# A decode step with grouped-query attention: the queries made the stationary operand of the scores, and 46 units of on-chip store in place of 48

## The chip, the cores and the metric

One core of one Trainium2 chip. The metric is the device time of one execution in microseconds (us), median of several executions. Most executions of one kernel here lie within 0.3 us of their median, so a difference of 1 us is well seen. All runs compared below are of the fast state, but for one single run that is named.

## The reference

One token goes through a block: a conditioned layer norm, attention over a cache of 65,536 positions, a second norm and a small gated feed-forward. The attention is all of the traffic: K and V have 8 heads x 65,536 x 128 in bf16, 134 MB each.

```
Hq, Hkv, Sk, Dh, D = 32, 8, 65536, 128, 512
q = x @ wq                              # 32 heads, 4 of them to one K/V head
scores = einsum('bhqd,bhkd->bhqk', q, k) * Dh ** -0.5
p = softmax(scores)
o = einsum('bhqk,bhkd->bhqd', p, v)
out = o.reshape(...) @ wo
# around it: h = layernorm(x)*(1+c)+s, x += g * attention(h); then x += g2 * swiglu(h2), F = 1792
```

## The kernel before

K and V come in chunks of 16,384 positions: 32 of K and 32 of V, 4 MB each, 128 partitions of 32 KB. They land in `store`, a hand-managed area of 4 KB units a partition; a chunk takes eight units, so 48 units are six slots. A load is issued, in a fixed order, when its slot comes free.

```
UNITS = 48
S_LAG = 2
...
const = ctx.enter_context(tc.tile_pool(name="const", bufs=1))
small = ctx.enter_context(tc.tile_pool(name="small", bufs=2))
once = ctx.enter_context(tc.tile_pool(name="once", bufs=1))
spool = ctx.enter_context(tc.tile_pool(name="store", bufs=1))
...
store = spool.tile([P, UNITS * UNIT], BF16, name="store", tag="store")
...
def room(n):          # n units that start at a multiple of n
    fits = [u for u in range(0, UNITS - n + 1, n) if all(free[u:u + n])]
    ...
```

A bank is 1,024 positions of K. TensorE turns it (four transposes of 128x128 words of 32 bits, each a pair of bf16), ACT and DVE in turn copy it out of PSUM, and eight small matmuls make the scores: a block of K is the stationary operand, 8 columns of q move.

```
def emit_T(n):
    ...
    for e4 in range(4):
        nc.tensor.transpose(out=ktp[:, e4, :], in_=kt32[:, j0:j0 + 2, :]..., identity=ident_f[:])
    ...                                      # copy to kts on ACT or DVE
    if jb == BPC - 1:
        done(("k", n // BPC))                # the slot is free, next load

def emit_S(n):
    ...
    for e4 in range(4):
        for e in range(2):
            nc.tensor.matmul(out=st[:, b0:b0 + 2, :]..., lhsT=ktsv[:, e4, :, e], rhs=qpair[:, g, e, :, :]...,
                             start=(e == 0), stop=(e == 1))

def sm_exp(cc, negb, h):                     # four times a chunk, once for each head
    nc.scalar.activation(out=pt_of[cc][:, :, h], in_=st_of[cc][:, :, h], func=ACT.Exp, ...)
```

PV is 32 matmuls a chunk with 512 columns of V moving, in four column tiles of TensorE at a time. At the end of the stream come w_gate, w_up and w_down, and after w_down has landed only 56 matmuls (`f_ps`), a few small instructions and the store of the result are left.

## Time and profile before

| | before |
|---|---|
| time, median of 13 runs (range) | 683.99 us (683.84 to 684.35) |
| DMA queue q1, share of 16 engines' span | 97.9% |
| instruction fetches (q8) | 64 |
| TensorE waiting for K | 60.3 us |
| chunk of K, issue to landing | 43.7 us |

From the page of before: span and instructions, the busy time of the engines, and two lines of the part on DMA queues (packets, MB, and the time that their packets took as a share of 16 engines' span).

```profile
span 682.3 us, 18421 instructions
...
PE 569.4 (83%) x8259; PEld 500.6 (73%) x8259; DVE 262.8 (39%) x612; ACT 201.3 (30%) x527; POOL 3.6 (1%) x17
...
q1 hardware_dynamic: 12160, 285.48, 97.9%
q8 instruction: 64, 1.05, 0.6%
```

The data queue q1 is at work for 97.9% of the span, on average over the 16 engines: 0.979 x 682.3 = 668.0 us. This product is how long an average engine was at the data itself. 285.48 MB in 668.0 us is 427 GB/s. What the stream could reach at most was not shown; but the packets of 32 KB, which carry 268 of the 285 MB, took 1221.0 ns on average and 1213 ns at the least, so by that measure only 0.7% is left in them (an estimate).

The table of stretches for before: start and end in us, their length, then busy us (and instructions) of each engine, the granted clock of TensorE, the mean busy share of the 16 DMA engines, GB/s.

```profile
core 0: us, PE busy (x) PEld busy (x) DVE busy (x) ACT busy (x) POOL busy (x), PEclk, DMA share, GB/s
20.00:660.00 640.00, 553.90 (x7877) 486.29 (x7878) 255.15 (x566) 197.74 (x520) 0.00 (x0) 0.85 1.00 428
...
665.00:677.00 12.00, 6.27 (x163) 5.80 (x159) 2.39 (x14) 0.42 (x2) 0.55 (x1) 0.50 0.55 224
```

From 20 to 660 us the mean share is 1.00: the DMA engines do not run dry. In the last 12 us it is 0.55: about half of the engines have finished, and the kernel waits for the others. That is the tail.

The waits of TensorE in before (engine, line, what it waited for: us in total, times, longest us), and the time of the K and V loads from issue to landing (KB each, median us):

```profile
PE ktp L336 <- DMA store<-in_A_k_cache_dram: 60.3, 26, 4.1
PE pvw L399 <- DMA store<-in_A_v_cache_dram: 9.3, 10, 2.6
```

```profile
store<-in_A_k_cache_dram SPq DMA_DIRECT2D x32, 4096.0 KB, 43.7
store<-in_A_v_cache_dram SPq DMA_DIRECT2D x31, 4096.0 KB, 51.7
```

TensorE waits for data, while the DMA engines always have a load at hand: loads queue for four to five times their own length.

The groups of instructions that the change replaces (line, engine, operation, out<-in, shapes, count | busy us, mean ns | idle before, releaser):

```profile
L357 PEld LDWEIGHTS <-kts 128*128 128x128 bf16 x4096 | 191.2, 102 | 16.7 <-ACT kts L340 1.5
L357 PE MATMUL st<-qpair,kts 128*128 128x8 bf16 x4096 | 183.7, 168 | 1.8 <-ACT kts L340 1.3
...
L389 ACT ACTIVATE pt<-st,negb 128x128 bf16<-128x128 f32 x128 | 51.3, 558 | 4.3 <-DVE negb L382 4.3
```

The last two waits for DMA in the timeline of before (start us, us, engine, line, operation, shapes, count, idle before and releaser):

```profile
673.54 1.97 PE L235 MATMUL gu_ps<-h2T,store 128*128 128x1 bf16 x56 [1.30 <-DMA store<-in_B_w_up_dram]
...
677.30 2.02 PE L604 MATMUL f_ps<-guT,store 128*128 128x1 bf16 x56 [0.63 <-DMA store<-in_B_w_down_dram]
```

So the end of the kernel is the landing of w_down plus 5 us.

### The profile page before, as it was taken

The page shows a single profiled execution, that of the slowest core. Times are in us where ns is not written, and L with a number is a line of the kernel's source. Part 1 is how long each engine was busy: PE and PEld are TensorE (multiplying, and loading weights), DVE is VectorE, ACT ScalarE, POOL GpSimd, SP SyncE. Part 2 cuts the span into 40 slices and gives each one's busy share as a digit, 9 for nine tenths or more (in the row PEclk, how much of TensorE's full clock was granted, in tenths as well). Part 3 has the DMA queues.
Part 4 walks back from the last instruction along what each step waited for, and adds up shares of the span by engine and source line. Part 5 has one row for each costly group of instructions (what it writes and reads, how often), then busy time and mean ns, then how long its engine had stood idle before and what let it go on. Part 6 is the DMA issues. An engine that isn't in the chain of part 4 may idle for free.

```text
span 682.3 us, 18421 instructions
## 1 busy us (share of the span) xinstructions
PE 569.4 (83%) x8259; PEld 500.6 (73%) x8259; DVE 262.8 (39%) x612; ACT 201.3 (30%) x527; POOL 3.6 (1%) x17
## 2 busy tenths in 40 slices
PE   1599789998898998988798889988998777989984
PEld 1588678886787887777687778866787666879864
DVE  2154335343343443434344333533444333435421
ACT  0053233333223333323233322322333312324320
POOL 1000000000000000000000000000000000000000
PEclk9998788788688886979969767989869888869965
DMA  9999999999999999999999999999999999999993
GB/s 377 437 429 428 425 433 430 426 429 425 432 434 427 428 426 430 431 429 432 426 431 426 429 431 426 431 429 429 431 428 425 429 426 421 432 426 428 423 410 155
DMA packets 12242, 286.65 MB, mean 420 GB/s; under 512 B 1282, under 2 KB 1796, under 8 KB 3332
## 3 DMA queue, kind: packets, MB, share of 16 engines
q1 hardware_dynamic: 12160, 285.48, 97.9%
q8 instruction: 64, 1.05, 0.6%
q14 instruction: 14, 0.11, 0.0%
q10 hardware_dynamic: 4, 0.00, 0.0%
HBM read 285.48 MB, written 0.00 MB: 418 GB/s over the span
## 4 chain that ended last, share of the span: by engine, by line
DMA 72%; PE 24%; DVE 2%; issue 0%; another core or an unknown queue 0%; SPq 0%; DVEq 0%
DMA store<-in_A_k_cache_dram 45%; DMA store<-in_A_v_cache_dram 19%; PE ktp L336 14%; DMA store<-in_B_w_down_dram 5%; PE st L357 4%; PE pvw L399 3%; DMA store<-in_A_wq_dram 3%; DVE kts L342 1%; DVE mx L364 1%; PE mb L379 1%; PE q_ps L235 1%; PE mt L369 0%; PE wo L516 0%; PE f_ps L604 0%
## 5 line engine op out<-in xcount | busy, mean ns | idle before, releaser
L336 PE MATMUL ktp<-ident_f,store 128*128 128x128 f32 x2048 | 387.6, 321 | 60.3 <-DMA store<-in_A_k_cache_dram 60.3
L336 PEld LDWEIGHTS ktp<-ident_f,store 128*128 128x128 f32 x2048 | 259.5, 162 | 88.2 <-issue 82.6
L342 DVE COPY kts<-ktp 128x512 int32<-128x512 int32 x256 | 177.0, 692 | 302.4 <-PE ktp L336 290.9
L340 ACT COPY kts<-ktp 128x512 f32<-128x512 f32 x256 | 151.4, 592 | 436.4 <-PE ktp L336 434.2
L357 PEld LDWEIGHTS <-kts 128*128 128x128 bf16 x4096 | 191.2, 102 | 16.7 <-ACT kts L340 1.5
L357 PE MATMUL st<-qpair,kts 128*128 128x8 bf16 x4096 | 183.7, 168 | 1.8 <-ACT kts L340 1.3
L399 PE MATMUL pvw<-store,pt 128*16 128x512 bf16 x960 | 65.4, 394 | 9.3 <-DMA store<-in_A_v_cache_dram 9.3
L389 ACT ACTIVATE pt<-st,negb 128x128 bf16<-128x128 f32 x128 | 51.3, 558 | 4.3 <-DVE negb L382 4.3
L399 PEld LDWEIGHTS <-pt 128*16 128x16 bf16 x960 | 19.9, 89 | 25.5 <-issue 11.3
L389 ACT ACTIVATION_READ_ACCUMULATOR pt<-st,negb 128x1 f32 x128 | 36.5, 285 | 0.0
L417 PE MATMUL oc<-sel,pvw_sb 128*128 128x4 f32 x240 | 32.4, 258 | 1.8 <-DVE pvw_sb L407 0.8
L417 PEld LDWEIGHTS oc<-sel,pvw_sb 128*128 128x128 f32 x240 | 29.9, 195 | 5.3 <-DVE pvw_sb L407 1.7
L407 DVE COPY pvw_sb<-pvw 128x512 f32<-128x512 f32 x30 | 20.8, 692 | 32.8 <-PE pvw L399 32.8
L235 PEld LDWEIGHTS <-store 128*128 128x128 bf16 x336 | 10.6, 112 | 15.5 <-DMA store<-in_A_wq_dram 8.5
L364 DVE TENSOR_REDUCE mx<-st 128x4 f32<-128x512 f32 x32 | 21.8, 681 | 0.5 <-PE st L357 0.5
L369 PE MATMUL mt<-ident_f,mx 128*4 128x128 f32 x32 | 10.5, 329 | 9.1 <-DVE mx L364 6.9
L379 PE MATMUL mb<-dg,mean_w 4*128 4x4 f32 x64 | 14.8, 300 | 0.1
L371 DVE TENSOR_REDUCE m<-mt 4x1 f32<-4x128 f32 x32 | 8.9, 279 | 13.5 <-PE mt L369 13.5
L379 PEld LDWEIGHTS mb<-dg,mean_w 4*128 4x128 f32 x64 | 12.0, 233 | 2.2 <-DVE dg L373 0.6
L369 PEld LDWEIGHTS mt<-ident_f,mx 128*4 128x4 f32 x32 | 2.6, 82 | 11.9 <-DVE mx L364 11.9
L419 DVE COPY oT<-oc 128x4 f32<-128x4 f32 x30 | 4.9, 162 | 16.4 <-PE oc L417 16.4
L235 PE MATMUL q_ps<-m_h,store 128*128 128x1 bf16 x128 | 3.6, 165 | 8.4 <-DMA store<-in_A_wq_dram 8.4
(109 smaller groups left out, 102.4 us busy)
## 6 DMA issues: line engine op xcount, KB each, us to landing
store<-in_A_k_cache_dram SPq DMA_DIRECT2D x32, 4096.0 KB, 43.7
store<-in_A_v_cache_dram SPq DMA_DIRECT2D x31, 4096.0 KB, 51.7
store<-in_A_wq_dram SPq DMA_DIRECT2D x1, 4096.0 KB, 19.5
store<-in_w_mod_dram SPq DMA_DIRECT2D x1, 3072.0 KB, 10.2
store<-in_A_wo_dram SPq DMA_DIRECT2D x3, 1024.0 KB, 49.3
store<-in_A_v_cache_dram SPq DMA_DIRECT2D x1, 2048.0 KB
store<-in_B_w_gate_dram SPq DMA_DIRECT2D x1, 1792.0 KB, 35.8
store<-in_B_w_up_dram SPq DMA_DIRECT2D x1, 1792.0 KB, 33.3
```

The source lines that it names most:

```text
L235: nc.tensor.matmul(out=out_ps[:, nb:nb + 1], lhsT=lhs(kc, nb), rhs=actT[:, kc:kc + 1], start=(kc == 0), stop=(kc == n_kc - 1))
L336: nc.tensor.transpose(out=ktp[:, e4, :], in_=kt32[:, j0:j0 + 2, :].rearrange("p a i -> p (a i)"), identity=ident_f[:])
L340: nc.scalar.copy(out=kts[:].bitcast(F32), in_=ktp[:])
L342: nc.vector.tensor_copy(out=kts[:].bitcast(I32), in_=ktp[:].bitcast(I32))
L357: nc.tensor.matmul(out=st[:, b0:b0 + 2, :].rearrange("p b h -> p (b h)"), lhsT=ktsv[:, e4, :, e], rhs=qpair[:, g, e, :, :].rearrange("p j ...
L364: nc.vector.tensor_reduce(out=mx[:], in_=st_of[cc][:].rearrange("p b h -> p h b"), axis=AX.X, op=ALU.max)
L369: nc.tensor.transpose(out=mt[:], in_=mx[:], identity=ident_f[:])
L379: nc.tensor.matmul(out=mb[:], lhsT=mean_w[0:rep, :], rhs=dg[:], start=True, stop=True)
L389: nc.scalar.activation(out=pt_of[cc][:, :, h], in_=st_of[cc][:, :, h], func=ACT.Exp, bias=negb[:, h:h + 1], scale=scale, accum_out=Lp[:, c ...
L399: nc.tensor.matmul(out=pvw[32 * jt:32 * jt + QB * rep, :], lhsT=pt_of[cc][:, b0:b0 + QB, :].rearrange("p b h -> p (b h)"), rhs=held[("v", ...
L407: nc.vector.tensor_copy(out=pvw_sb[:], in_=pvw[:])
L417: nc.tensor.matmul(out=oc_ps[:], lhsT=pvw_sb[:, bl * Dh:(bl + 1) * Dh], rhs=sel[:, bl, :], start=(bl == 0), stop=(bl == QB - 1))
```

## The change

Its intent is to cut the work of TensorE and ACT: with q as the stationary operand, K moves 512 columns at a time, in four column tiles, and 1,024 pairs of weight load and matmul replace 4,096. The scores then lie with (position, head) on the partitions, so that one exponential a chunk does for four, but the probabilities have to be turned back with four transposes. Pools are resized for it, and the store loses two units.

```
-UNITS = 48
+UNITS = 46
...
-    ktspool = ctx.enter_context(tc.tile_pool(name="ktspool", bufs=3))
+    ktspool = ctx.enter_context(tc.tile_pool(name="ktspool", bufs=7))
+    pepool = ctx.enter_context(tc.tile_pool(name="pepool", bufs=1))
...
+    ident_bf = const.tile([P, P], BF16, name="ident_bf", tag="ident_bf")
-    mean_w = const.tile([P, P], F32, name="mean_w", tag="mean_w")
+    mean_1 = const.tile([P, 1], F32, name="mean_1", tag="mean_1")
+    mean_w = mean_1[:].broadcast_to([P, P])
...
-    pvw_sb = const.tile([P, QB * Dh], F32, name="pvw_sb", tag="pvw_sb")
+    pvw_sb = const.tile([P, QB // 2 * Dh], F32, name="pvw_sb", tag="pvw_sb")
...
+    qw = const.tile([P, 2, 2, 2 * QW - SL], BF16, name="qw", tag="qw")
...
+    def emit_S(banks):                  # four banks at a time
+        for e in range(2):
+            for n in banks:
+                ...
+                slot, jt = divmod(i, 4)
+                nc.tensor.matmul(out=st_of[cc][32 * jt:32 * jt + QW, :],
+                                 lhsT=qw[:, cc // NCPH % 2, e, at_q:at_q + QW],
+                                 rhs=kts_of[n][:].rearrange("q f (p e) -> q (f p) e", e=2)[:, :, e],
+                                 start=(slot == 0 and e == 0), stop=(slot == BPC // 4 - 1 and e == 1),
+                                 tile_position=(0, 32 * jt), skip_group_check=True)
...
+    def sm_exp(cc, negb):               # one exponential a chunk
+        nc.scalar.activation(out=pe[:], in_=st_of.pop(cc)[:], func=ACT.Exp, bias=negb[:], ...)
+    def sm_back(cc, pe):
+        for e4 in range(4):
+            nc.tensor.transpose(out=tp[:, e4, :], in_=pe[:, e4 * P:(e4 + 1) * P], identity=ident_bf[:])
+        nc.vector.tensor_copy(out=pt_of[cc][:], in_=tp[:])
...                                      # PV reads another layout; its fold is done in two halves;
...                                      # PV of chunk 30 in tiles like the others, not block by block
```

More of the change, by code (lines that the diff above doesn't have):

```diff
@@ L193 @@
     _make_identity(nc, ident_f[:])
-    mean_w = const.tile([P, P], F32, name="mean_w", tag="mean_w")
-    nc.vector.memset(mean_w[:], 1.0 / D)
+    ident_bf = const.tile([P, P], BF16, name="ident_bf", tag="ident_bf")
+    nc.vector.tensor_copy(out=ident_bf[:], in_=ident_f[:])
+    mean_1 = const.tile([P, 1], F32, name="mean_1", tag="mean_1")
+    nc.vector.memset(mean_1[:], 1.0 / D)
+    mean_w = mean_1[:].broadcast_to([P, P])
     mhalf = const.tile([P, 1], F32, name="mhalf", tag="mhalf")
@@ L244, in layernorm_in @@
         tot_ps = pmisc.tile([P, 1], F32, name="ln1_tot", tag="misc")
-        nc.tensor.matmul(out=tot_ps[:], lhsT=mean_w[:], rhs=rs[:], start=True, stop=True)
+        nc.tensor.matmul(out=tot_ps[:], lhsT=mean_w, rhs=rs[:], start=True, stop=True)
         negmean = once.tile([P, 1], F32, name="ln1_nm", tag="ln_nm")
@@ L253, in layernorm_in @@
         var_ps = pmisc.tile([P, 1], F32, name="ln1_var", tag="misc")
-        nc.tensor.matmul(out=var_ps[:], lhsT=mean_w[:], rhs=rs2[:], start=True, stop=True)
+        nc.tensor.matmul(out=var_ps[:], lhsT=mean_w, rhs=rs2[:], start=True, stop=True)
         ve = once.tile([P, 1], F32, name="ln1_ve", tag="ln_ve")
@@ L326, in head_stats @@
         if g not in heads:
-            heads[g] = tuple(stat.tile([P, NCPH, rep], F32, name=f"{n}{g}", tag=n) for n in ("Mb", "Lp", "oT"))
+            heads[g] = tuple(stat.tile([P, NCPH, k], F32, name=f"{n}{g}", tag=n)
+                             for n, k in (("Mb", rep), ("Lp", 1), ("oT", rep)))
         return heads[g]
@@ L345, in emit_T @@
             done(("k", n // BPC))
-    def emit_S(n):
-        cc, i = divmod(n, BPC)
-        if i == 0:
-            st_of[cc] = pst.tile([P, NB, rep], F32, name=f"st_{cc}", tag="st")
-        st = st_of[cc]
-        ktsv = kts_of.pop(n)[:].rearrange("q f (p e) -> q f p e", e=2)
-        g = cc // NCPH
-        for e4 in range(4):
-            b0 = i * 8 + 2 * e4
-            for e in range(2):
-                nc.tensor.matmul(out=st[:, b0:b0 + 2, :].rearrange("p b h -> p (b h)"),
-                                 lhsT=ktsv[:, e4, :, e],
-                                 rhs=qpair[:, g, e, :, :].rearrange("p j h -> p (j h)"),
-                                 start=(e == 0), stop=(e == 1))
+    QW = 8 * rep
@@ new lines, with set_q @@
+    SL = 2 * rep
+    qw = const.tile([P, 2, 2, 2 * QW - SL], BF16, name="qw", tag="qw")
+    nc.vector.memset(qw[:], 0.0)
+    def set_q(g):
+        nc.vector.tensor_copy(out=qw[:, g % 2, :, QW - SL:QW], in_=qpair[:, g, :, :, :].rearrange("p e j h -> p e (j h)"))
+    def emit_S(banks):
+        for e in range(2):
+            for n in banks:
+                cc, i = divmod(n, BPC)
+                if i == 0 and e == 0:
+                    st_of[cc] = pst.tile([P, 4 * P], F32, name=f"st_{cc}", tag="st")
+                slot, jt = divmod(i, 4)
+                at_q = QW - SL - slot * SL
+                nc.tensor.matmul(out=st_of[cc][32 * jt:32 * jt + QW, :],
[3 more added lines that the diff above has]
+                                 tile_position=(0, 32 * jt), skip_group_check=True)
+        for n in banks:
+            del kts_of[n]
@@ L362, in sm_max @@
     def sm_max(cc):
-        mx = small.tile([P, rep], F32, name=f"mx_{cc}", tag="mx")
-        nc.vector.tensor_reduce(out=mx[:], in_=st_of[cc][:].rearrange("p b h -> p h b"), axis=AX.X, op=ALU.max)
+        mx = small.tile([P, 1], F32, name=f"mx_{cc}", tag="mx")
+        nc.vector.tensor_reduce(out=mx[:], in_=st_of[cc][:], axis=AX.X, op=ALU.max)
         return mx
     def sm_turn(cc, mx):
-        mt = pmisc.tile([rep, P], F32, name=f"mt_{cc}", tag="misc")
+        mt = pmisc.tile([1, P], F32, name=f"mt_{cc}", tag="misc")
@@ L369, in sm_turn @@
         nc.tensor.transpose(out=mt[:], in_=mx[:], identity=ident_f[:])
-        m4 = small.tile([rep, 1], F32, name=f"m4_{cc}", tag="m4")
-        nc.vector.tensor_reduce(out=m4[:], in_=mt[:], axis=AX.X, op=ALU.max)
-        dg = small.tile([rep, rep], F32, name=f"dg_{cc}", tag="dg")
-        nc.vector.tensor_scalar(out=dg[:], in0=ident_f[0:rep, 0:rep], scalar1=m4[:], scalar2=float(D), op0=ALU.mult, op1=ALU.mult)
-        return dg
-    def sm_spread(cc, dg):
+        m4 = small.tile([1, rep], F32, name=f"m4_{cc}", tag="m4")
@@ L377, in sm_spread @@
+        nc.vector.tensor_reduce(out=m4[:], in_=mt[:].rearrange("o (r h) -> o h r", h=rep), axis=AX.X, op=ALU.max)
+        return m4
+    def sm_spread(cc, m4):
         Mb = head_stats(cc // NCPH)[0]
         mb = pmisc.tile([P, rep], F32, name=f"mb_{cc}", tag="misc")
-        nc.tensor.matmul(out=mb[:], lhsT=mean_w[0:rep, :], rhs=dg[:], start=True, stop=True)
-        nc.vector.tensor_copy(out=Mb[:, cc % NCPH, :], in_=mb[:])
-        negb = small.tile([P, rep], F32, name=f"negb_{cc}", tag="negb")
@@ L382, in sm_spread @@
-        nc.vector.tensor_scalar(out=negb[:], in0=mb[:], scalar1=-scale, scalar2=None, op0=ALU.mult)
+        nc.tensor.matmul(out=mb[:], lhsT=mean_w[0:1, :], rhs=m4[:], start=True, stop=True)
+        mine = small.tile([P, rep], F32, name=f"mine_{cc}", tag="mine")
+        nc.vector.scalar_tensor_tensor(out=mine[:], in0=mb[:], scalar=-scale * D, in1=at4[:], op0=ALU.mult, op1=ALU.mult)
+        negb = small.tile([P, 1], F32, name=f"negb_{cc}", tag="negb")
+        nc.vector.reduce_sum(out=negb[:], in_=mine[:], axis=AX.X)
@@ L383, in sm_spread @@
+        nc.vector.tensor_scalar(out=Mb[:, cc % NCPH, :], in0=mb[:], scalar1=float(D), scalar2=None, op0=ALU.mult)
         return negb
-    def sm_exp(cc, negb, h):
+    def sm_exp(cc, negb):
         Lp = head_stats(cc // NCPH)[1]
-        if h == 0:
-            pt_of[cc] = ptpool.tile([P, NB, rep], BF16, name=f"pt_{cc}", tag="pt")
-        nc.scalar.activation(out=pt_of[cc][:, :, h], in_=st_of[cc][:, :, h], func=ACT.Exp,
-                             bias=negb[:, h:h + 1], scale=scale, accum_out=Lp[:, cc % NCPH, h:h + 1])
-        if h == rep - 1:
-            del st_of[cc]
+        pe = pepool.tile([P, 4 * P], BF16, name=f"pe_{cc}", tag="pe")
+        nc.scalar.activation(out=pe[:], in_=st_of.pop(cc)[:], func=ACT.Exp,
+                             bias=negb[:], scale=scale, accum_out=Lp[:, cc % NCPH, :])
+        return pe
@@ L394 @@
+    def sm_back(cc, pe):
+        tp = pmisc.tile([P, 4, P], BF16, name=f"tp_{cc}", tag="misc")
+        for e4 in range(4):
+            nc.tensor.transpose(out=tp[:, e4, :], in_=pe[:, e4 * P:(e4 + 1) * P], identity=ident_bf[:])
+        pt_of[cc] = ptpool.tile([P, 4, P], BF16, name=f"pt_{cc}", tag="pt")
+        nc.vector.tensor_copy(out=pt_of[cc][:], in_=tp[:])
     NQ = NB // QB
     def pv_one(cc, q4):
-        b0 = QB * q4
-        jt = q4 % 4
+        s2, r = divmod(q4, 16)
+        e4, jt = divmod(r, 4)
+        v5 = held[("v", cc)].rearrange("p (s t f a) d -> p s t f (a d)", t=4, f=4, a=2)
+        c0 = 32 * jt + 2 * SL * s2
@@ L399, in pv_one @@
         nc.tensor.matmul(out=pvw[32 * jt:32 * jt + QB * rep, :],
-                         lhsT=pt_of[cc][:, b0:b0 + QB, :].rearrange("p b h -> p (b h)"),
-                         rhs=held[("v", cc)][:, b0:b0 + QB, :].rearrange("p j d -> p (j d)"),
+                         lhsT=pt_of[cc][:, e4, c0:c0 + QB * rep],
+                         rhs=v5[:, 2 * s2:2 * s2 + 2, jt, e4, :],
                          start=(q4 < 4), stop=(q4 >= NQ - 4),
@@ L406, in pv_one @@
             del pt_of[cc]
-            nc.vector.tensor_copy(out=pvw_sb[:], in_=pvw[:])
+            nc.vector.tensor_copy(out=pvw_sb[:], in_=pvw[:, 0:QB // 2 * Dh])
     def pv_run(cc, a, b):
@@ L411, in pv_run, with pv_fold @@
             pv_one(cc, q4)
-    def pv_fold(cc):
-        oT = head_stats(cc // NCPH)[2]
-        oc_ps = pmisc.tile([P, rep], F32, name=f"oc_{cc}", tag="misc")
-        for bl in range(QB):
-            nc.tensor.matmul(out=oc_ps[:], lhsT=pvw_sb[:, bl * Dh:(bl + 1) * Dh], rhs=sel[:, bl, :],
-                             start=(bl == 0), stop=(bl == QB - 1))
-        nc.vector.tensor_copy(out=oT[:, cc % NCPH, :], in_=oc_ps[:])
+    def pv_fold(cc, oc_ps):
+        last_half = oc_ps is not None
+        if not last_half:
+            oc_ps = pmisc.tile([P, rep], F32, name=f"oc_{cc}", tag="misc")
+        for i in range(QB // 2):
+            bl = i + last_half * QB // 2
+            nc.tensor.matmul(out=oc_ps[:], lhsT=pvw_sb[:, i * Dh:(i + 1) * Dh], rhs=sel[:, bl, :],
+                             start=(bl == 0), stop=(bl == QB - 1))
+        if last_half:
+            nc.vector.tensor_copy(out=head_stats(cc // NCPH)[2][:, cc % NCPH, :], in_=oc_ps[:])
+        else:
+            nc.vector.tensor_copy(out=pvw_sb[:], in_=pvw[:, QB // 2 * Dh:])
+        return oc_ps
     def pv_direct(cc):
@@ L425, in pv_direct @@
         for b in range(NB):
-            nc.tensor.matmul(out=oc_ps[:], lhsT=v[:, b, :], rhs=pt[:, b, :], start=(b == 0), stop=(b == NB - 1))
+            slot, jt, e4, jj = b // 32, b // 8 % 4, b // 2 % 4, b % 2
+            c0 = 32 * jt + SL * slot + rep * jj
+            nc.tensor.matmul(out=oc_ps[:], lhsT=v[:, b, :], rhs=pt[:, e4, c0:c0 + rep], start=(b == 0), stop=(b == NB - 1))
         done(("v", cc))
@@ L434, in head_weights @@
         Lt_ps = pmisc.tile([P, NCPH, rep], F32, name=f"Lt{g}", tag="misc")
-        nc.tensor.matmul(out=Lt_ps[:].rearrange("p c h -> p (c h)"), lhsT=mean_w[:],
-                         rhs=Lp[:].rearrange("p c h -> p (c h)"), start=True, stop=True)
+        lm = small.tile([P, NCPH, rep], F32, name=f"lm{g}", tag="lm")
+        nc.vector.tensor_tensor(out=lm[:], in0=Lp[:].broadcast_to([P, NCPH, rep]),
+                                in1=at4[:].unsqueeze(1).broadcast_to([P, NCPH, rep]), op=ALU.mult)
+        nc.tensor.matmul(out=Lt_ps[:].rearrange("p c h -> p (c h)"), lhsT=mean_w,
+                         rhs=lm[:].rearrange("p c h -> p (c h)"), start=True, stop=True)
         mg = small.tile([P, rep], F32, name=f"mg{g}", tag="mg")
@@ L459, in head_out @@
         nc.vector.tensor_reduce(out=og[:], in_=ow[:].rearrange("p c h -> p h c"), axis=AX.X, op=ALU.add)
-        om = once.tile([P, rep, NQ4], BF16, name=f"om{g}", tag="om")
-        nc.vector.tensor_tensor(out=om[:], in0=og[:].unsqueeze(2).broadcast_to([P, rep, NQ4]),
+        om = pepool.tile([P, 4 * P], BF16, name=f"om{g}", tag="pe")
+        om = om[:, 0:P].rearrange("p (h q) -> p h q", h=rep)
+        nc.vector.tensor_tensor(out=om, in0=og[:].unsqueeze(2).broadcast_to([P, rep, NQ4]),
                                 in1=of[:].unsqueeze(1).broadcast_to([P, rep, NQ4]), op=ALU.mult)
@@ L466, in head_turn @@
         of_ps = pmisc.tile([P, rep], F32, name=f"of{g}", tag="misc")
-        nc.tensor.matmul(out=of_ps[:], lhsT=om[:].rearrange("p h q -> p (h q)"), rhs=at4_bf[:], start=True, stop=True)
+        nc.tensor.matmul(out=of_ps[:], lhsT=om.rearrange("p h q -> p (h q)"), rhs=at4_bf[:], start=True, stop=True)
         nc.vector.tensor_copy(out=oF[:, g, :], in_=of_ps[:])
@@ L488 @@
         at(e + 2, keep(("nb", cc), lambda dg, cc=cc: sm_spread(cc, dg), ("dg", cc)))
-        for h in range(rep):
-            at(e + 3 + h // 2, lambda cc=cc, h=h: sm_exp(cc, carry[("nb", cc)], h))
+        at(e + 3, keep(("pe", cc), lambda nb, cc=cc: sm_exp(cc, nb), ("nb", cc)))
+        at(e + 4, lambda cc=cc: sm_back(cc, carry.pop(("pe", cc))))
         g = cc // NCPH
@@ L499 @@
         if cc == NCH - 2:
-            at(END + 5, lambda cc=cc: pv_direct(cc))
-            continue
+            runs = [END + 5, END + 5]
         for step, (_, a, b) in zip(runs, PV_RUNS):
@@ L504 @@
         p1 = runs[-1] + 1
-        at(p1, lambda cc=cc: pv_fold(cc))
+        at(p1, keep(("oc", cc), lambda cc=cc: pv_fold(cc, None)))
+        at(p1 + 1, lambda cc=cc: pv_fold(cc, carry.pop(("oc", cc))))
         if cc % NCPH == NCPH - 1:
-            at(p1 + 1, keep(("om", g), lambda wgt, g=g: head_out(g, wgt), ("wgt", g)))
-            at(p1 + 2, lambda g=g: head_turn(g, carry.pop(("om", g))))
+            at(p1 + 2, keep(("om", g), lambda wgt, g=g: head_out(g, wgt), ("wgt", g)))
+            at(p1 + 3, lambda g=g: head_turn(g, carry.pop(("om", g))))
+            if g + 2 < Hkv:
+                at(e + 2, lambda g=g: set_q(g + 2))
     def wo_part(g0, g1):
@@ L526 @@
         at((NCH - len(wo_groups) + i) * BPC + 9, lambda p=p: wo_part(*p))
+    for g in range(min(2, Hkv)):
+        set_q(g)
     last = max(side)
@@ L530 @@
             emit_T(n)
-        if 0 <= n - S_LAG < NBANKS:
-            emit_S(n - S_LAG)
+        if 0 <= n - S_LAG < NBANKS and (n - S_LAG) % 4 == 3:
+            emit_S(range(n - S_LAG - 3, n - S_LAG + 1))
         for fn in side.get(n, ()):
@@ L569 @@
     ms_ps = pmisc.tile([P, 3], F32, name="ms_ps", tag="misc")
-    nc.tensor.matmul(out=ms_ps[:], lhsT=mean_w[:], rhs=ys[:], start=True, stop=True)
+    nc.tensor.matmul(out=ms_ps[:], lhsT=mean_w, rhs=ys[:], start=True, stop=True)
     ve2 = once.tile([P, 1], F32, name="ve2", tag="ve2")
```

## The prediction

> **What bounds the kernel now.** DMA. The page's queue part gives q1 285.48 MB and 97.9% of 16 engines' span; the table of stretches shows DMA share 1.00 and 428 GB/s from 20 to 660 us. TensorE is not the limit: PE 83% busy, waiting 60.3 us for K and 9.3 us for V (waits view). K loads land 43.7 us after issue, while one 4 MB load takes 4.19 MB / 428 GB/s = 9.8 us: a load may be issued some 34 us late before DMA runs dry.
>
> The end is set by the slower half of the DMA engines. By 1-us stretches DMA share falls from 1.0 to about 0.55 at 665 us and stays there until 677 us: eight engines finish 12 us after the others, with equal packets. The last load (w_down) lands at 677.2 and the chain ends 5 us later. I put the lag down to instruction fetches: the page shows q8 "instruction", 64 packets, 1.05 MB[...]. In the DMA records their durations repeat with period 8, as if eight engines took them in turn: 12 us / 8 = 1.5 us each (1.07 us of transfer[...]). That only eight engines serve them is my inference.
>
> **What the change does.** Scores: 4096 K-stationary pairs (8 columns) become 1024 pairs with q stationary, K moving by 512, four column tiles at once. Before, eight pairs cost about 0.19 us per bank (timeline: steps of 0.675 us against 0.49 us for four transposes), 97 us in all. PV shows what tiled 512-column matmuls cost: 16 in 1.0 us. Eight per four banks thus cost 0.5 to 0.7 us with switching: 65 to 90 us. With four added bf16 transposes per chunk, TensorE time hardly falls: PE 75 to 85%. ACT loses three of four Exp (0.56+0.28 us each), to roughly 130 us; DVE gains a back-copy, up to 0.69 us per chunk, to about 280 us. All this is off the path.
>
> UNITS 48 to 46 leaves five, not six, 4 MB slots (near the end four, since wo_last needs another block). Slack falls from 34 to about 24 us, near the end to 5 to 12 us: estimates from 14 to 18 us of K processing. That should just hold.
>
> TensorE instructions fall by about 6060 of 16518: some 24 of 64 fetches vanish, three per slow engine, 3 x 1.5 us = about 4.5 us from the end.
>
> **Prediction.** 684.0 - 4.5 = 679.5 us; range 677.0 to 684.0. Faster by over 2%: 0.02; within 2%: 0.94; slower: 0.04.
>
> **What would show the steps right.** q8 about 40 packets; q1 share 97 to 98%; DMA share 1.00 to 660 us and a half-share tail of about 7 us instead of 12; K issue-to-landing about 34 us; ACT 130 us. Wrong: fetches gone but the tail unchanged means the lag has another cause.
>
> **What would make it wrong.** Starvation: if TensorE stays at half clock (the table shows 0.50 in stretches such as 340-350 us, a step costing 1.15 instead of 0.675 us), a chunk takes over 20 us; with fewer slots DMA would show shares below 1 and the time could pass 700 us. Strided K as moving operand, or mode switching, could cost more than PV shows. The four-slot end could stall v30 and v31.

The sum came to 684.0 - 4.5 = 679.5 us. Its 24 fetches follow from the page of before alone: 64 packets for 16,518 weight loads and matmuls, so 6,060 fewer are 23.5 packets. Its 1.5 us for each is an estimate, 12 us of tail / 8 fetches an engine; of this only the transfer (1.07 us, the mean of the 64 packets) was read from the trace.

## The result, and the profile after

| | before | after |
|---|---|---|
| time, median (range) | 683.99 us (683.84 to 684.35) | 676.41 us (676.13 to 676.61) |
| ratio, 95% interval | | 0.9888 (0.9878 to 0.9898) |

(An eighth execution of after, 677.06 us, is not among the seven of this median.) A ratio is the mean time of one kernel's fast runs over that of the other's of the same rounds, so it is not quite the ratio of the medians quoted. The time falls by 7.6 us, 1.1%. The prediction said 4.5 us and gave 677.0 as its lower end: the direction and the class (within 2%) held, the size did not, and the time lies 0.6 us outside its range.

The page of after, the same lines:

```profile
span 674.3 us, 12261 instructions
...
PE 541.3 (80%) x5227; PEld 368.5 (55%) x5227; DVE 281.5 (42%) x694; ACT 178.5 (26%) x335; POOL 3.6 (1%) x17
...
q1 hardware_dynamic: 12160, 285.48, 98.6%
q8 instruction: 41, 0.67, 0.4%
```

The table of stretches for after, columns as before:

```profile
20.00:660.00 640.00, 531.30 (x5009) 359.27 (x5009) 276.24 (x663) 176.85 (x332) 0.00 (x0) 0.88 1.00 431
...
663.00:669.00 6.00, 3.72 (x105) 3.48 (x102) 0.44 (x3) 0.21 (x1) 0.00 (x0) 0.50 0.58 233
```

Two things have changed, and the second was not foreseen. The tail with half of the engines busy lasts about 6.5 us (663 to 669.4) and not 12, as predicted, with 41 fetches and not 64. But the stream itself is faster as well: 431 GB/s and not 428 at the same DMA share of 1.00, and the tail begins 2 us earlier. The product of share and span says it too: 0.986 x 674.3 = 664.9 us of data time an engine, against 668.0, for exactly the same 12160 packets and 285.48 MB. Fewer instruction fetches explain only a part of that. They are another queue, but a data packet that meets a fetch takes longer (of the 32 KB packets over 1400 ns, 73 of 74 before and 50 of 51 after overlap one in time; they took 1717 and 1691 ns on average, against a median of 1215 and 1213); in the packets' records that part is 0.8 of the 3.1 us.

The waits, the loads, the groups and the end of the timeline of after:

```profile
PE ktp L341 <- DMA store<-in_A_k_cache_dram: 73.3, 29, 4.9
...
PE pvw L420 <- DMA store<-in_A_v_cache_dram: 3.4, 4, 2.3
```

```profile
store<-in_A_k_cache_dram SPq DMA_DIRECT2D x32, 4096.0 KB, 41.4
store<-in_A_v_cache_dram SPq DMA_DIRECT2D x31, 4096.0 KB, 33.3
```

```profile
L368 PE MATMUL st<-kts,qw 128*32 128x512 bf16 x1024 | 92.5, 435 | 0.2 <-DVE kts L347 0.2
...
L368 PEld LDWEIGHTS <-qw 128*32 128x32 bf16 x1024 | 16.7, 96 | 26.0 <-issue 26.0
...
L402 ACT ACTIVATE pe<-st,negb 128x512 bf16<-128x512 f32 x32 | 22.2, 694 | 4.1 <-DVE Mb L396 4.1
L409 PEld LDWEIGHTS <-pe 128*128 128x128 bf16 x128 | 8.0, 104 | 27.9 <-ACT pe L402 27.9
L409 PE MATMUL tp<-ident_bf,pe 128*128 128x128 bf16 x128 | 13.9, 238 | 10.1 <-ACT pe L402 10.0
```

```profile
665.71 1.97 PE L239 MATMUL gu_ps<-h2T,store 128*128 128x1 bf16 x56 [1.22 <-DMA store<-in_B_w_up_dram]
...
669.36 2.02 PE L641 MATMUL f_ps<-guT,store 128*128 128x1 bf16 x56 [0.52 <-DMA store<-in_B_w_down_dram]
```

The scores' matmuls took 183.7 us of PE and take 92.5, and their weight loads 191.2 and take 16.7. Nothing of this reaches the end: TensorE waits 13 us longer for K. The chain from the landing of w_down is what it was (5 us); w_down simply lands 7.9 us earlier (677.30 to 669.36).

What made the data packets faster? The records of the single DMA packets answer how, not why. There are 8,192 packets of 32 KB (one partition of one chunk), 512 an engine:

```
                 mean ns   median   1214 ns or less   over 1400 ns
before           1221.0    1215     49%               74 packets
after            1216.0    1213     99%               51 packets
```

After, practically each packet takes 1213 ns, but for the few that share their engine with a fetch (over 1400 ns; q14 has 14 small fetches of its own in both kernels). Before, half of the packets lie 2 to 20 ns above. 5.0 ns x 512 = 2.6 us an engine. The size of this jitter was compared with what TensorE, ACT and DVE did during each packet; no group of instructions shows any relation to it (all correlations are below 0.1). So it was likely something that holds all the time.

### The profile page after: what moved, and what is told of

Its sections match the earlier page's. It is cut to its first block, busy times and chain, and to the rows that moved or that the text cites. A ratio compares the mean times of both kernels' runs of the same rounds, so it can differ in the third digit from the quotient of the medians.

```text
span 674.3 us, 12261 instructions
## 1 busy us (share of the span) xinstructions
PE 541.3 (80%) x5227; PEld 368.5 (55%) x5227; DVE 281.5 (42%) x694; ACT 178.5 (26%) x335; POOL 3.6 (1%) x17
## 3 DMA queue, kind: packets, MB, share of 16 engines
q1 hardware_dynamic: 12160, 285.48, 98.6%
HBM read 285.48 MB, written 0.00 MB: 423 GB/s over the span
## 4 chain that ended last, share of the span: by engine, by line
DMA 71%; PE 24%; ACT 2%; DVE 2%; issue 1%; SPq 0%; DVEq 0%; ACTq 0%
DMA store<-in_A_k_cache_dram 55%; PE ktp L341 15%; DMA store<-in_A_v_cache_dram 10%; DMA store<-in_B_w_down_dram 5%; PE pvw L420 3%; PE st L368 3%; ACT pe L402 1%; DVE kts L347 1%; ACT kts L345 1%; PE tp L409 1%; DVE mx L378 1%; PE mb L391 1%; PE oc L440 1%; PE mt L383 0%; PE wo L551 0%
## 5 line engine op out<-in xcount | busy, mean ns | idle before, releaser
L341 PE MATMUL ktp<-ident_f,store 128*128 128x128 f32 x2048 | 330.3, 306 | 73.3 <-DMA store<-in_A_k_cache_dram 73.3
L368 PE MATMUL st<-kts,qw 128*32 128x512 bf16 x1024 | 92.5, 435 | 0.2 <-DVE kts L347 0.2
L428 DVE COPY pvw_sb<-pvw 128x256 f32<-128x256 f32 x31 | 13.2, 425 | 46.3 <-PE pvw L420 46.3
L368 PEld LDWEIGHTS <-qw 128*32 128x32 bf16 x1024 | 16.7, 96 | 26.0 <-issue 26.0
L378 DVE TENSOR_REDUCE mx<-st 128x1 f32<-128x512 f32 x32 | 22.0, 687 | 4.3 <-PE st L368 4.3
L402 ACT ACTIVATE pe<-st,negb 128x512 bf16<-128x512 f32 x32 | 22.2, 694 | 4.1 <-DVE Mb L396 4.1
L409 PE MATMUL tp<-ident_bf,pe 128*128 128x128 bf16 x128 | 13.9, 238 | 10.1 <-ACT pe L402 10.0
L411 DVE COPY pt<-tp 128x512 bf16<-128x512 bf16 x32 | 13.6, 424 | 19.7 <-PE tp L409 19.7
L391 PEld LDWEIGHTS mb<-m,mean 1*128 1x128 f32 x64 | 11.7, 227 | 8.0 <-issue 5.6
L391 PE MATMUL mb<-m,mean 1*128 1x4 f32 x64 | 14.5, 295 | 0.0
## 6 DMA issues: line engine op xcount, KB each, us to landing
store<-in_A_k_cache_dram SPq DMA_DIRECT2D x32, 4096.0 KB, 41.4
store<-in_A_v_cache_dram SPq DMA_DIRECT2D x31, 4096.0 KB, 33.3
```

Of the source, the lines that this page charges most:

```text
L368: nc.tensor.matmul(out=st_of[cc][32 * jt:32 * jt + QW, :], lhsT=qw[:, cc // NCPH % 2, e, at_q:at_q + QW], rhs=kts_of[n][:].rearrange("q f ...
L378: nc.vector.tensor_reduce(out=mx[:], in_=st_of[cc][:], axis=AX.X, op=ALU.max)
L391: nc.tensor.matmul(out=mb[:], lhsT=mean_w[0:1, :], rhs=m4[:], start=True, stop=True)
L402: nc.scalar.activation(out=pe[:], in_=st_of.pop(cc)[:], func=ACT.Exp, bias=negb[:], scale=scale, accum_out=Lp[:, cc % NCPH, :])
L409: nc.tensor.transpose(out=tp[:, e4, :], in_=pe[:, e4 * P:(e4 + 1) * P], identity=ident_bf[:])
L411: nc.vector.tensor_copy(out=pt_of[cc][:], in_=tp[:])
```

## The experiments

Each was compared with before on its own chip, where before took 683.98 to 684.01 us throughout.

**Before again, pairs added to after, half of the scores, five slots.** The first question was whether the jitter belongs to the kernel at all, and what a fetch costs. The edits:

```
e1: none
e2 (after, in emit_T, ahead of the transposes):
+        for _ in range(3):
+            nc.tensor.matmul(out=ktp[0:1, 0, 0:1], lhsT=ident_bf[:, 0:1], rhs=ident_bf[:, 0:1], start=True, stop=True)
e3 (before, in emit_S; the result is wrong on purpose):
-            for e in range(2):
+            for e in range(1):
-                                 start=(e == 0), stop=(e == 1))
+                                 start=True, stop=True)
e4 (before):
-UNITS = 48
+UNITS = 46
```

> The kernel before, unchanged, to see what repeats in its profile. In the first profile of before, the 32 KB packets took 1221.0 ns on average, against 1216.0 ns in the profile of after (512 such packets an engine, so 2.6 us an engine). Theory 'the kernel stretches the packets': the average is again near 1221 ns, and most packets lie 2 to 12 ns above 1213. Rival 'another chip or another hour': here nearly all are 1213 ns and the average is near 1217 ns. The time must be 684.0 either way, ratio 1.000.

> After, with three added one-column pairs of weight load and matmul per bank: 1536 pairs, 3072 instructions, 12 fetches more (41 to 53), nearly no operand read. Theory A, a fetch costs its engine 1.7 us and only the slower eight engines pay: 12 / 8 x 1.7 = +2.6 us, 679.0 us. Theory B, the whole gain of 7.6 us is the 23 fetches, 0.33 us each: +4.0 us, 680.4 us. Rival C, operand reads of the scores' weight loads or the slots made the gain and not the fetches: 676.4 us, no change.

> Before, with the second half (e = 1) of each score sum left out; the result is wrong on purpose. 2048 pairs fewer, 16 fetches fewer (64 to 48), and half of the reads of K as weights gone. A: 16 / 8 x 1.7 = -3.4 us, 680.6 us. B: 16 x 0.33 = -5.3 us, 678.7 us. C: half of the gain, about 680.2 us. Together with e2, A and B give the same slope per fetch in both runs; C gives none in e2.

> Before with UNITS 46 alone, so five slots and not six. A and B: 684.0 us, same; K issue to landing falls from 43.7 us to about 34. Rival, 'the other slot layout and the shorter queue give the part of the gain that the fetches do not': about 681.5 us. If the shorter queue starves DMA: above 685 us with DMA shares below 1 before 660 us.

| run | time, median us | change from its parent | fetches | 32 KB packets, mean ns | 1214 ns or less |
|---|---|---|---|---|---|
| e1, before again | 684.01 | 0.0 | 64 | 1221.0 | 51% |
| e2, after, pairs everywhere | 682.81 | +6.4 | 53 | 1217.3 | 99% |
| e3, before, half of the scores | 681.01 | -3.0 | 48 | 1220.1 | 48% |
| e4, before, five slots | 683.86 | -0.1 | 64 | 1221.0 | 51% |

e1: the jitter belongs to the kernel; the profile repeats to 0.1 ns. e4: neither the number of slots nor the shorter queue matters. e3: 16 fetches fewer give 3.0 us, near the 3.4 of theory A, and the jitter stays although half of the reads of K as weights is gone; which speaks against the kind of score matmul as its cause (e6 and e9 below settle it).

e2 missed all three expectations, and its stretches say why:

```profile
620.00:630.00 10.00, 9.94 (x123) 6.99 (x123) 4.36 (x13) 3.18 (x7) 0.00 (x0) 1.00 0.99 424
630.00:635.00 5.00, 5.00 (x58) 3.30 (x56) 2.23 (x4) 1.76 (x3) 0.00 (x0) 1.00 0.77 298
```

TensorE is busy without a break, and from 630 to 635 us the DMA share falls to 0.77: a load was issued too late. This is the starvation that the prediction feared for the end, where wo_last takes a part of one slot and four are left. Its one run of 686.51 us (the others lie at 682.62 to 682.95) may be the same stall, longer. So e2 measures a stall and says little of fetches. It does show that after holds its narrow end only while TensorE has some room.

**The start address.** One thing that holds all the time and differs between the two kernels is where `store` lies. The built programs' memory maps give it: the pools ahead of it have shrunk, by the tiles that the diff resizes, so that it starts at byte 22944 of each partition before and at 22016 after. 22016 = 86 x 256; 22944 is 160 bytes past a multiple of 256. All slots lie at multiples of 4 KB from there, so each packet shares its remainder. The four next runs test that, and the fetches again with room for TensorE; and one of them asks which DMA engines lag. A tile that nobody reads moves the store (and the pools behind it by the same bytes; of these, only the store is a target of DMA):

```
e5 (before) and e6 (after):
+    padpool = ctx.enter_context(tc.tile_pool(name="pad", bufs=1))
+    pad = padpool.tile([P, 8], F32, name="pad", tag="pad")       # 32 bytes
+    nc.vector.memset(pad[:], 0.0)
     spool = ctx.enter_context(tc.tile_pool(name="store", bufs=1))
e7 (after):
+        for _ in range(3 if n < 24 * BPC else 0):
+            nc.tensor.matmul(...)                                # as in e2
e8 (after): the large load of w_down in pieces
-        nc.sync.dma_start(out=<128 partitions>, in_=...)
+        nc.sync.dma_start(out=dst[0:64], in_=src[0:64])
+        nc.sync.dma_start(out=dst[64:128, 0:1], in_=src[64:128, 0:1])
+        nc.sync.dma_start(out=dst[64:128, 1:nf], in_=src[64:128, 1:nf])
```

> Before with a 32-byte tile put ahead of the 4 MB slots, so that they start at byte 22976 of a partition (a multiple of 64) and not at 22944 (32 over a multiple of 64). Nothing else changes; 64 fetches stay. Theory 'start address': the packets of 32 KB fall to 1213 ns but for those that meet a fetch, the average from 1221 to about 1217.5 ns, which over 512 packets and the smaller ones is 2 us an engine: 682.0 us. Rival 'the kind of work (ACT's four strided exponentials, K as weights) stretches the packets': no change, 684.0 us and 1221 ns.

> After with a 32-byte tile ahead of the slots: they start at byte 22048 and not at 22016. Theory 'start address': packets 2 to 12 ns longer as in before, about +2.3 us, 678.7 us. Rival: 676.4 us, no change.

> After with the three added one-column pairs per bank in chunks 0 to 23 alone, since the earlier run with all chunks overloaded TensorE near the end, where slots are few: 1152 pairs, 2304 instructions, 9 fetches more (41 to 50). With the slope that the run with half scores showed, 3.0 us / 16 = 0.19 us per fetch: +1.7 us, 678.1 us, DMA share 1.00 up to 660 us, tail longer by as much. Slope 0.33 us (all of the gain): +3.0 us, 679.4 us. Rival without fetches: 676.4 us.

> After with the large load of w_down split into partitions 0 to 63 (768 KB) and partitions 64 to 127 (256 and 512 KB), to see which DMA engines lag. If the lagging eight serve one half of the partitions, the loads of the two halves land some 6 to 7 us apart; if they are spread over both, all land together near 669 us. Time near 676.4 us.

| run | store starts at | time, median us | change from its parent | fetches | 32 KB packets, mean ns | 1214 ns or less |
|---|---|---|---|---|---|---|
| e5, before + 32 bytes | 22976 (multiple of 64) | 684.46 | +0.5 | 64 | 1221.4 | 20% |
| e6, after + 32 bytes | 22048 (multiple of 32) | 680.25 | +3.8 | 41 | 1220.9 | 10% |
| e7, after, pairs in chunks 0 to 23 | 22016 | 678.95 | +2.5 | 50 | 1216.5 | 99% |
| e8, after, w_down in halves | 22016 | 683.44 (one run, state unknown) | +7.0 | 41 | 1215.9 | 99% |

e6 is the clearest run: nothing but 32 unused bytes, and half of the gain is gone. Its page:

```profile
span 678.5 us, 12262 instructions
...
q1 hardware_dynamic: 12160, 285.48, 98.4%
q8 instruction: 41, 0.67, 0.4%
```

41 fetches as in after, but 0.984 x 678.5 = 667.6 us of data time an engine as in before. e5 missed: a multiple of 64 is not enough.

e7: nine fetches more cost 2.5 us, between the two slopes (1.7 and 3.0) and more for each fetch than e3 shows (0.28 and not 0.19 us). The DMA share stayed at 1.00 from 20 to 660 us, so this is no stall. Eight engines take turns with the fetches (shown further below), and the last engine sets the landing. By their start times, 40 of the 41 fetches of after begin before w_down has landed, five to an engine, and 49 of the 50 of e7, so that one engine has seven. Two more on that engine, at about 1.4 us each, are 2.8 us: an estimate, near the 2.5 measured.

e8 failed as an experiment. These are its stretches, before and at the halves:

```profile
20.00:655.00 635.00, 533.79 (x4921) 360.44 (x4922) 275.67 (x656) 176.39 (x331) 0.00 (x0) 0.87 1.00 431
659.00:664.00 5.00, 0.62 (x3) 0.50 (x2) 1.63 (x9) 0.21 (x1) 0.55 (x1) 0.50 1.05 227
```

All 16 engines are busy and move 227 GB/s and not 431. Some are at the load to 64 partitions (packets of 4 KB, about 300 ns each and not 159 as in after), the others still at w_gate and w_up (14 KB, about 1050 ns and not 535). Why these packets took twice as long was not shown. The run cost 7 us and did not tell which engines lag.

**How much alignment, and do the two terms add?** To make room for larger pads these runs have 46 units, which alone changed nothing (e4). The edits are the pad of e5, with 96, 352 and 224 bytes:

```
e9, e10, e11 (before):
-UNITS = 48
+UNITS = 46
+    pad = padpool.tile([P, 24], ...)     # e9: 96 bytes; e10: 88 for 352 bytes; e11: 56 for 224 bytes
e12 (after):
-    pvw_sb = const.tile([P, QB // 2 * Dh], F32, ...)
+    pvw_sb = const.tile([P, QB // 2 * Dh], BF16, ...)
-    sel = const.tile([P, QB, rep], F32, ...)
+    sel = const.tile([P, QB, rep], BF16, ...)
-        m4 = small.tile([1, rep], F32, ...)
+        m4 = small.tile([1, rep], BF16, ...)
...                                       # and the constant 1/D in bf16 for that matmul
```

> Before with UNITS 46 (which alone changed nothing) and a 96-byte tile ahead, so that the 4 MB slots start at byte 23040 = 45 x 512. 64 fetches stay. Theory 'two terms that add': the start address is worth what it cost after when it was spoilt, 680.25 - 676.4 = 3.85 us, so 680.2 us, packets at 1213 ns but for those that meet a fetch. Rival 'the start address matters only with the other scores': 684.0 us and packets near 1221 ns.

> The same with 352 bytes: slots start at 23296, a multiple of 256 and not of 512. If 256 suffices: 680.2 us. If it takes 512: 684.0 us.

> The same with 224 bytes: slots start at 23168, a multiple of 128 and not of 256. A multiple of 64 (22976) did not help. If 128 suffices: 680.2 us; if not: 684.0 us, packets 2 to 12 ns above 1213.

> After with bf16 in place of fp32 in the folds of PV and in the spreading of the maximum, so that each is one pass and not two: 156 pairs fewer, 312 instructions, 39 or 40 fetches and not 41; the slots start at 21504 = 42 x 512. Fetches at 0.16 to 0.28 us each: 676.4 - 0.3 = 676.1 us; up to 1 us less if the one engine that serves six fetches and not five ends the kernel. Rival: no change.

| run | store starts at | time, median us | change from its parent | fetches | 32 KB packets, mean ns | 1214 ns or less |
|---|---|---|---|---|---|---|
| e9, before | 23040 = 90 x 256 (45 x 512) | 680.66 | -3.3 | 64 | 1218.0 | 98% |
| e10, before | 23296 = 91 x 256 | 680.85 | -3.1 | 64 | 1217.5 | 99% |
| e11, before | 23168 = 90.5 x 256 | 684.03 | 0.0 | 64 | 1221.2 | 42% |
| e12, after, fewer passes | 21504 = 84 x 256 | 676.34 | -0.1 | 40 | 1216.0 | 99% |

Of the starts that were tried, a multiple of 128 (e11, 684.03 us) or of 64 (e5, 684.46 us) gains nothing, one of 256 gains all (e10, 680.85 us), and one of 512 adds nothing that is seen (e9, 680.66 us). The page of e9, with the scores and the fetches of before:

```profile
span 678.8 us, 18424 instructions
...
q1 hardware_dynamic: 12160, 285.48, 98.1%
q8 instruction: 64, 1.05, 0.5%
```

0.981 x 678.8 = 665.9 us of data time. With e6 there are now all four corners:

| median us | store off a multiple of 256 | store on one | worth of the address |
|---|---|---|---|
| 64 fetches (scores of before) | 684.0 (before) | 680.66 (e9) | 3.3 |
| 41 fetches (scores of after) | 680.25 (e6) | 676.41 (after) | 3.8 |
| worth of the new scores | 3.7 | 4.25 | |

The two terms add, within 0.6 us, to the 7.6 us of the change.

e12 tried to beat both kernels with fewer instructions still (half of a fold of PV is four matmuls of `oc<-sel,pvw_sb` in the timeline of after, in fp32, and two in that of e12, in bf16), and gave no difference that is seen: 676.34 against 676.41 us. Its count fell by one fetch only, which at 0.16 to 0.28 us is hardly above the spread; by turns, the engines that end last still have five each. So there is no version here that beats after; but before with 46 units and 96 idle bytes gets 3.3 of the 7.6 us.

## Why the prediction was wrong in size

- **The bound: right.** DMA share 1.00 from 20 to 660 us in both kernels; TensorE waits for K longer than before (60.3 to 73.3 us).
- **Score work off the path: right.** PE 80% of the span (75 to 85 was said), DVE 281.5 us (280). ACT was mis-sized: 178.5 us and not 130. The prediction counted 0.56 + 0.28 us for each exponential; but these overlap, busy time counts overlapping records once, and the groups show only 51.3 us for the exponentials (128 of 558 ns would be 71.4 us one after another), of which 22.2 remain. That DVE came out exact is in part luck: the copy back takes 0.42 us a chunk (13.6 us in all) and not up to 0.69, and the fold in two halves added copies of its own (20.8 us before, 26.1 after).
- **The tail and the fetches: right, and nearly so in size.** "TensorE instructions fall by about 6060 of 16518: some 24 of 64 fetches vanish ... about 4.5 us from the end": 23 vanished, and with the start address held the same the new scores gave 3.7 us (off) and 4.25 us (on). The half-share tail of "about 7 us instead of 12" came as 6.5. A packet of the instruction queue goes with some 255 weight loads and matmuls: 64 packets of 16 KB for 16,518 of them before (258 each), 41 for 10,454 after (255). e3 supports fetches as the cause within one kind of scores (16 fewer, 3.0 us); e6 and before differ in more than fetches. That eight engines serve them was an inference in the prediction, and the DMA records of e9 bear it out, where nearly all packets are equally long. Each packet can be put on the engine where another has just ended (within 12 ns). Up to 517 us all 47 fetches then fall into gaps of 0.86 to 1.03 us on eight of the 16 engines, in turn but for a few swaps, and none on the other eight; the eight have moved 411 to 413 packets of 32 KB by then, the others 417 to 419. With the data packet that it stretches by some 0.5 us (1691 and not 1213 ns in after), a fetch of some 0.9 us costs its engine about 1.4 us. From e9 to after, 64 to 40 fetches before the landing are three fewer an engine: 4.2 us as an estimate, 4.25 measured. With the store off a multiple of 256 the same three gave only 3.7 us; why is open.
- **The slots: harmless, as said, for another reason than said.** K loads did not fall to 34 us from issue to landing (41.4); it was V that did (51.7 to 33.3). The fewer slots alone do this: e4 has 42.1 and 33.8. e2 shows how near the four-slot end is to a stall.
- **The step that failed is the sum itself: "684.0 - 4.5".** It has no term for the address of the store. The prediction read "UNITS 48 to 46" and the pools as a matter of how many loads may wait, and not as a move of every DMA destination by 928 bytes. That term measures 3.3 us (e9) and 3.8 us (e6). On an engine it is made of 3.4 to 4.8 ns for each of 512 packets that meet no fetch (1.7 to 2.5 us), some 0.5 us in the smaller packets, and somewhat shorter fetches (1.07 to 0.94 us each, so about 1.1 us on an engine with eight and 0.7 on one with five). The sums, 3.3 and 3.7 us, are estimates from the records and near what was measured. It is not part of the idea of the change at all: it came along by luck of the tile sizes.

What stays open: why a start off a multiple of 256 costs 2 to 12 ns in some packets and nothing in others; and which eight engines serve the fetches.

## What to carry to other kernels

When DMA is never idle, look at what else uses the engines and at how long each packet takes: compare the product of queue share and span between two kernels that move the same bytes, since a difference there is packet time and not scheduling (packets that a fetch stretches are part of it). Put large DMA destinations at a multiple of 256 bytes in the partition (worth 3.3 to 3.8 us of 684 here, e9 and e6; why is open), and check that address again after any change of the tiles ahead of them. On a stream-bound kernel, fewer TensorE instructions can pay although TensorE is not the limit: here 16 fetches fewer gave 3.0 us (e3), and the fetches took turns on eight of the DMA engines that carry the data (e9).
